# A causal convolution and a SwiGLU block in one kernel: one unit more with its convolution on ACT, DVE and POOL instead of PE, and a cast, its transposes and some copies issued sooner

## The chip, the cores and the metric

One core of a Trainium2 chip. The time is the device time of the kernel in microseconds; each changed version was run four times and the median is quoted. Ratios compare a kernel's runs with those of the kernel before in the same rounds, with a 95% interval in brackets; they are not quite the ratio of the quoted medians. A verdict of faster or slower needs 2%. The engines are named as in the profile: PE does matmuls, ACT activations, DVE and POOL elementwise work; SP issues transfers.

## The reference

A depthwise causal convolution of 7 taps (8 heads, softmax over a head's taps), then a SwiGLU block on 32768 tokens of 192 channels with 1536 hidden channels.

```python
# x: (8, 4096, 192), weight: (8, 7)
w = softmax(weight)                       # per head
out = einsum('hk,bskhg->bshg', w, windows_of_7(x))      # causal, 24 channels a head
g   = out @ w_gate                        # (32768, 192) @ (192, 1536)
y   = (silu(g) * (out @ w_val)) @ w_out   # -> (32768, 192)
```

## The kernel before

The tokens are cut into 16 units of 2048, a unit into 4 blocks of 512, a block into 12 steps of 128 hidden channels. A step is six gate/val matmuls, a SiLU on ACT, a product on DVE, and the matmuls back, which lag behind. `n` counts steps, 48 to a unit. The engines run side by side; the helper `seq` holds each of them to the order in which the program lists its instructions, step by step.

The matmuls want the convolved tokens with channels on partitions (`xc[b]`, three tiles). There are two ways to get them. Units that are not in `POOLED` have their convolution on PE (`cv` matmuls with a band matrix), and their result goes out to memory (`scr<-tm`) and back through transposing transfers. (Unit 0 has a start of its own, alike in both kernels.) Units in `POOLED` are *channel-major*:

```python
POOLED = (2, 4, 5, 6, 8, 9, 10, 12, 13, 14, 15)
...
def cast_x(u):            # POOL issues it: x to fp16 in memory, one transfer for the unit
    ... nc.gpsimd.dma_start(out=flat[...], in_=bass.AP(tensor=x_flat.tensor, ...))
def turn_x(u, i, at):     # SP issues it: the transposes that bring it in
    ... nc.sync.dma_start_transpose(out=t, in_=rows[:, at : at + P])
# a job: tap 0 and 3 on ACT, taps 1 and 2 on DVE, taps 4 to 6 and the other additions on POOL
FIRST, ON_DVE, ON_ACT, ON_POOL = 0, (1, 2), (3,), (4, 5, 6)
...
def place(u, i):          # SP issues it: the four copies that put a block's channels in place
    for dst, src in ((t1[0:Q], t0[Q:P]), (t1[Q:P], y), (t2[0:Q], y), (t2[Q:P], t0[0:Q])):
        seq(nc.sync.dma_start(out=dst, in_=src))
```

(The last lines are shortened: every slice also takes columns 0 to 511.) A unit has six jobs: a "block" job makes `pxc0` of a block, a "pair" job makes `y` for two blocks. I call the four copies a block's *slot*. Where each of these stands in the program is set by step numbers:

```python
def planned(v):
    s0 = ustep * v                        # first step of the unit, ustep = 48
    ...
    else:
        late = 12 if v == 4 else 0
        cast, jobs = s0 - 112 + late, s0 - 89
        times = range(cast + 7, cast + 27, 2)      # the eight transposes and two joins
...
# in pooled_work: a slot is placed once its jobs are done, some steps later
done = max(finished[job] for job in need)
if n < max(done + (14 if u == 2 else 18), ustep * u + NCH * i - 16):
    break
```

SP issues nearly everything that matters here from one queue: results out, transposes in, slots, `scr` writes and fetches.

## Time and profile before

| | before |
|---|---|
| median of all runs beside the change | 795.3 us (793.57 to 796.49) |
| span in the profile | 792.6 us |
| PE busy | 98% |
| one block of 512 tokens at PE's pace | 11.73 us |

The page's groups tell what one channel-major job costs. Columns: line, engine, operation, output<-inputs, shapes, count; then busy time and mean ns of one; then idle time of the engine before them.

```profile
L630 POOL TENSOR_TENSOR total<-total,piece 128x512 f32<-128x512 f32 x132 | 178.3, 1351 | 11.0
L645 POOL TENSOR_SCALAR piece<-x,both_taps 128x512 f32<-128x512 f16 x198 | 164.8, 832 | 0.0
L655 DVE SCALAR_TENSOR_TENSOR total<-x,both_taps,total 128x512 f32<-128x512 f16 x132 | 138.9, 1052 | 0.0
```

66 jobs: 3 products and 4 additions each on POOL, 2 steps on DVE. POOL carries most of it, about 8 us a job. The prediction below shows the waits and timelines.

### The profile page before, as it was taken

The numbers are of one execution on the slowest core, as the hardware profiler recorded it, in microseconds if no ns is written. First come the engines' busy times: TensorE is split into PE (matmuls) and PEld (weight loads), VectorE is DVE, ScalarE is ACT, GpSimd is POOL, SyncE is SP. The second block draws the span as 40 slices with busy tenths as digits, with TensorE's granted clock in tenths as the row PEclk, the third lists the DMA queues.
The fourth block names the chain that finished last, engine by engine and source line by source line (L and its number), as shares of the span: only waits on it lengthen the run. The fifth ranks groups of instructions, "written<-read, shape, count | busy, mean of one in ns | idle before, by whom it ended". The sixth has DMA issues, their size and how long they took to land.

```text
span 792.6 us, 27857 instructions
## 1 busy us (share of the span) xinstructions
PE 775.1 (98%) x11307; PEld 620.7 (78%) x11307; DVE 675.1 (85%) x1018; ACT 584.7 (74%) x999; POOL 551.2 (70%) x523
## 2 busy tenths in 40 slices
PE   8999999599999999999999999999999999999997
PEld 5766666477788888769889888868888888888886
DVE  6687998579999987799999997789999999997775
ACT  6666787478788876778877885687887787876664
POOL 8100797749999992069999998029999999997000
PEclk9999999889999999999999999999999999999999
DMA  9959825655352277565545219548644345221211
GB/s 135 181 121 143 159 65 108 133 126 101 75 120 79 68 109 146 117 139 99 116 96 110 65 43 181 127 112 130 117 95 107 92 92 113 69 58 45 68 55 42
DMA packets 154471, 82.38 MB, mean 104 GB/s; under 512 B 98110, under 2 KB 153798, under 8 KB 153798
## 3 DMA queue, kind: packets, MB, share of 16 engines
q1 hardware_dynamic: 136422, 64.26, 36.4%
q0 software_dynamic: 17920, 16.34, 14.1%
q8 instruction: 88, 1.44, 0.8%
q14 instruction: 41, 0.34, 0.1%
HBM read 32.68 MB, written 38.34 MB: 90 GB/s over the span
## 4 chain that ended last, share of the span: by engine, by line
PE 95%; POOL 2%; DVE 1%; DMA 1%; ACT 0%; issue 0%; SPq 0%; DVEq 0%; POOLq 0%
PE val L773 37%; PE acc L799 31%; PE gate L773 25%; POOL total L630 1%; DVE h L784 1%; PE warm L874 1%; POOL piece L645 1%; DMA pxc<-pxc 1%; PE cv L476 0%; PE turn L445 0%; PE cv L387 0%; SPq L704 0%; PE acc L820 0%; DVE total L655 0%; POOL pxc L630 0%
## 5 line engine op out<-in xcount | busy, mean ns | idle before, releaser
L782 ACT ACTIVATE sig<-gate 128x512 f16<-128x512 f32 x768 | 458.4, 597 | 189.6 <-PE gate L773 130.5
L784 DVE TENSOR_TENSOR h<-sig,val 128x512 f16<-128x512 f16 x768 | 502.6, 686 | 107.0 <-PE gate L773 65.8
L773 PEld LDWEIGHTS <-w 64*128 64x128 f16 x4608 | 354.0, 110 | 129.6 <-issue 15.5
L773 PE MATMUL gate<-pxc,w 64*128 64x512 f16 x1584 | 373.3, 377 | 9.3 <-DMA pxc<-pxc 9.2
L773 PE MATMUL val<-pxc,w 64*128 64x512 f16 x1584 | 372.4, 377 | 0.6 <-DMA pxc<-pxc 0.2
L799 PE MATMUL acc<-wo,h 64*128 64x192 f16 x6096 | 328.4, 243 | 0.5 <-issue 0.4
L799 PEld LDWEIGHTS <-h 64*128 64x128 f16 x6096 | 301.3, 94 | 28.8 <-issue 2.8
L630 POOL TENSOR_TENSOR total<-total,piece 128x512 f32<-128x512 f32 x132 | 178.3, 1351 | 11.0
L773 PE MATMUL val<-xc,w 64*128 64x512 f16 x720 | 169.6, 376 | 0.8 <-DVE h L784 0.7
L773 PE MATMUL gate<-xc,w 64*128 64x512 f16 x720 | 169.8, 376 | 0.0
L645 POOL TENSOR_SCALAR piece<-x,both_taps 128x512 f32<-128x512 f16 x198 | 164.8, 832 | 0.0
L655 DVE SCALAR_TENSOR_TENSOR total<-x,both_taps,total 128x512 f32<-128x512 f16 x132 | 138.9, 1052 | 0.0
L630 POOL TENSOR_TENSOR total<-total,part 128x512 f32<-128x512 f32 x66 | 90.7, 1375 | 66.5 <-DVE total L655 66.4
L630 POOL TENSOR_TENSOR pxc<-total,piece 128x512 f16<-128x512 f32 x44 | 58.1, 1320 | 3.7
L504 POOL COPY tm<-tm 128x1280 f16<-128x1280 f16 x4 | 5.0, 1250 | 67.2 <-DVE tm L493 67.2
L680 ACT ACTIVATE total<-x,both_taps 128x512 f32<-128x512 f16 x66 | 47.1, 714 | 0.7 <-DMA x<-xs 0.7
L680 ACT ACTIVATE part<-x,both_taps 128x512 f32<-128x512 f16 x66 | 47.1, 714 | 0.0
L858 DVE COPY o_sb<-acc 128x384 f32<-128x384 f32 x63 | 34.7, 551 | 0.0
L630 POOL TENSOR_TENSOR y<-total,piece 128x512 f16<-128x512 f32 x22 | 29.5, 1342 | 1.8
L857 ACT COPY o_sb<-acc 128x384 f32<-128x384 f32 x63 | 30.3, 480 | 0.2
L98 POOL DMA_DIRECT2D x<-in_x_dram x10 | 8.7, 884 | 24.4 <-ACT sig L782 24.4
L493 ACT CAST tm<-cv 128x480 f16<-128x480 f32 x16 | 8.2, 562 | 5.6 <-PE cv L476 5.6
(67 smaller groups left out, 85.8 us busy)
## 6 DMA issues: line engine op xcount, KB each, us to landing
out_dram<-o_sb SPq DMA_DIRECT2D x63, 384.0 KB
pxc<-pxc SPq DMA_DIRECT2D x88, 64.0 KB
pxc<-y SPq DMA_DIRECT2D x88, 64.0 KB
xs<-in_x_dram POOLq DMA_DIRECT2D x7, 768.0 KB, 7.0
x<-in_x_dram POOLq DMA_DIRECT2D x10, 480.0 KB, 10.4
scr<-tm SPq DMA_DIRECT2D x28, 130.0 KB
xs<-in_x_dram POOLq DMA_DIRECT2D x4, 774.0 KB, 8.1
x<-x SPq DMA_DIRECT2D x6, 480.0 KB
```

Source lines behind the costliest of these rows:

```text
L98: nc.gpsimd.dma_start(out=t[p0 + i0 : p0 + i1, w0 - at : w1 - at, :], in_=bass.AP(tensor=x_flat.tensor, offset=(t0 + size * w0 - pad + i0) ...
L493: eng(tm[u][:, NG * r : NG * r + NG, 2 * grp * hp : 2 * grp * hp + 2 * grp].rearrange("p g (t e) -> p g t e", t=2), banks[r][:, 0 : 2 * w] ...
L630: nc.gpsimd.tensor_tensor(job["dst"] if k == K - 1 else total, total, part, op=ALU.add)
L645: nc.gpsimd.tensor_scalar(part, shifted(k), scalar1=job["tap"][:, k : k + 1], scalar2=1.0, op0=ALU.mult, op1=ALU.mult,)
L655: nc.vector.scalar_tensor_tensor(job["total"], shifted(k), job["tap"][:, k : k + 1], job["total"], op0=ALU.mult, op1=ALU.add,)
L680: nc.scalar.activation(part, shifted(k), AF.Copy, scale=job["tap"][:, k : k + 1])
L773: nc.tensor.matmul(o, w16[m][p0 : p0 + Q, k, e::E], xc[b][k][p0 : p0 + Q, 0:TB], start=(k == 0), stop=(k == SL - 1),)
L782: silu[n] = seq(nc.scalar.activation(sg, g, AF.Silu)).ins
L784: seq(nc.vector.tensor_tensor(hj, sg, v, op=ALU.mult))
L799: nc.tensor.matmul(acc[b][bank][:, s, :], hj[p0 : p0 + Q, ts(2 * bank + s, P)], wo16[p0 : p0 + Q, j, :], start=(not second and j == 0 and ...
L857: seq(nc.scalar.copy(o_sb[:, 0:2, :], acc[b][0]))
L858: seq(nc.vector.tensor_copy(o_sb[:, 2:4, :], acc[b][1]))
```

## The change

The intent is to have less convolution on PE, the busiest engine (units 1, 3 and 8 instead of 1, 3, 7 and 11), and to bring unit 2's slots to PE in time. It does the latter by placing them sooner and by no longer holding back the cast and transposes of unit 4. All casts but unit 2's come three steps sooner (unit 4's fifteen, with the delay of twelve that goes).

```diff
-    POOLED = (2, 4, 5, 6, 8, 9, 10, 12, 13, 14, 15)
+    POOLED = (2, 4, 5, 6, 7, 9, 10, 11, 12, 13, 14, 15)
@@ planned
-            late = 12 if v == 4 else 0
-            cast, jobs = s0 - 112 + late, s0 - 89
-            times = range(cast + 7, cast + 27, 2)
+            cast, jobs = s0 - 115, s0 - 89
+            times = range(s0 - 105, s0 - 85, 2)
@@ pooled_work
-            if n < max(done + (14 if u == 2 else 18), ustep * u + NCH * i - 16):
+            if n < max(done + (12 if u == 2 else 18), ustep * u + NCH * i - 16):
```

## The prediction

> **What bounds the kernel now.** I read the page first, then the table of waits, then the timelines of PE, SP and POOL around the longest wait, and last the times of the conv matmuls. The page shows one engine full and the others not:
>
> ```profile
> PE 775.1 (98%) x11307; PEld 620.7 (78%) x11307; DVE 675.1 (85%) x1018; ACT 584.7 (74%) x999; POOL 551.2 (70%) x523
> ```
>
> In the timeline of ACT, the gate activations (L782) that open a block of 512 tokens are 11.73 us apart in almost the whole trace (from 232.89 to 244.62, for one). That is the PE's own pace; 64 blocks at it are 64 x 11.73 = 750.7 us, so only 792.6 - 750.7 = 41.9 us can be had without touching the matmuls of the FFN. Most is start and end. The rest I found by subtracting the usual step from each step: unit 2 (blocks 8 to 11) has 14 us of it, each unit with its conv on PE about 1.4, and three steps lose 0.3 to 0.9 each. The table of waits names the big one:
>
> ```profile
> PE gate L773 <- DMA pxc<-pxc: 9.2, 2, 8.7
> SPq L605 <- DMA xs<-in_x_dram: 56.2, 6, 13.5
> ```
>
> The timeline of PE shows where, and that the matmuls after it are slower (0.58 us against 0.38):
>
> ```profile
> 148.44 0.38 PE L773 MATMUL val<-pxc,w 64*128 64x512 f16 x1
> 157.49 0.58 PE L773 MATMUL gate<-pxc,w 64*128 64x512 f16 x1 [8.68 <-DMA pxc<-pxc]
> ```
>
> This is unit 2's last block. Its slot copies (L704) stand on SP's queue behind other things, as the timeline of SP shows:
>
> ```profile
> 110.09 0.58 SPq L704 DMA_DIRECT2D pxc<-pxc  x1
> 122.73 1.31 SPq L605 DMA_TRANSPOSE x<-xs  x1
> ...
> 142.99 1.27 SPq L605 DMA_TRANSPOSE x<-xs  x1
> 144.36 5.48 SPq L512 DMA_DIRECT2D scr<-tm  x8
> 149.88 5.05 SPq L520 DMA_DIRECT2D scr<-tm  x1
> 155.04 0.95 SPq L704 DMA_DIRECT2D pxc<-pxc  x1
> 156.03 1.23 SPq L704 DMA_DIRECT2D pxc<-y  x2
> 157.31 0.60 SPq L704 DMA_DIRECT2D pxc<-pxc  x1
> ```
>
> SP idles from 110.7 to 122.7, until the cast of unit 4 has landed (POOL issues it at 116.13); then it works through unit 4's transposes to 144.3, sends out unit 3's conv, is held 5.05 us in one issue that takes 0.39 to 0.45 us elsewhere, and only then reaches the slot. POOL had finished that slot's data at 134.0. The cast of unit 5 was issued at 147.88, so it was in flight during the 5.05 us.
>
> **What the Trainium skill says.** *DMA: Bandwidth & Descriptors*, "Anatomy of one DMA": "any semaphore wait happens on the issuing sequencer before dispatch", so a transfer that waits holds all behind it on its queue. The trace agrees: SP idles 12.0 us ahead of the first transpose. The same page, "Issuing engines are not separate DMA queues": transfers of all issuers share the 16 DMA engines and interleave. The 5.05 us beside a cast agree, though they do not prove it. *TensorE: Matmul & The Clock Gate*, Part 1: after an idle window of about 3.4 us the array falls to half rate, and it takes about as long to come back. The trace agrees: 0.58 to 0.63 us a matmul for some 5 us after the 8.68 us gap, and none after short gaps. *GPSIMD Engine Reference*, 3.1: a two-input operation has a floor from one read port. The trace has 1.35 us for the POOL addition against 0.83 us for its one-input product; this is why a channel-major unit costs POOL so much.
>
> **The change part by part.**
>
> 1. *One conv unit less on PE* (1, 3, 7, 11 become 1, 3, 8). It takes away 64 cv matmuls, two groups of 32 (L476), and 8 evictions. Unit 6, which holds the conv of unit 7, has blocks of 12.55 and 12.37 us instead of 11.73: 0.82 + 0.64 = 1.46 us; unit 10 has 0.78 + 0.64 = 1.42 us. Saved: **1.4 us**.
>
> 2. *One more channel-major unit.* Six jobs. DVE gains 12 x 1.05 = 12.6 us and loses 4 x 0.65; ACT gains 12 x 0.71 = 8.6 and loses 4 x 0.56. Neither bounds a block in a unit that has such jobs now (11.73 us throughout), so 0. POOL gains 6 x (2 x 1.35 + 1.38 + 1.33 + 3 x 0.83) = 47.4 us plus 0.6 for the cast, lying beside PE; but the order matters, see 4.
>
> 3. *Transposes and cast of unit 4 sooner, slots of unit 2 two steps sooner.* By the order of instructions, the cast of unit 4 now stands on POOL right after the first y (99.9 us in the trace of before) instead of after the third pxc (116.2). It can be issued at 100, land at 107 (median to landing 7.6 us, the one at 116.13 took 6.6), and SP starts unit 4's transposes 15 us earlier. From 107 I add SP's own durations in the new order (before, transposes and one slot took 122.73 to 144.3, 21.6 us): slot of block 9 issued at about 114 to 116, slot of block 10 at 128 to 130, all transposes done by 128. The conv write-out is then bound by its evictions (135), not by SP; eight issues and the ninth take 5.3 us as at other units, so slot 11 is issued at 140.5 to 143 and landed at 145, against about 147 when PE wants it. The cast of unit 5 follows job 4.0 on POOL, at about 146, after the write-out. So both waits go: block 10's steps 120 and 121 lose 1.11 + 0.44, block 11's steps 132 to 134 lose 10.24 + 0.93 + 1.06, of which the last two are the slow clock: **13.8 us**, with perhaps 1 left over. Without the earlier cast the two steps of placing alone would not do it.
>
> 4. *Casts three steps sooner.* For all later units the cast still stands on POOL after the first job of the unit before, by the order; on POOL this part moves nothing. That is the trouble: in channel-major units in a row, POOL is slower than PE. First jobs of units 12, 13, 14 start at 531.8, 581.7 and 630.7, 15 at 680.6: 49.6 us a unit against 4 x 11.73 = 46.9, so each cast comes about 2.5 us later against PE than the one before. The timelines of POOL and SP show what hangs on it:
>
> ```profile
> 589.72 0.55 POOL L590 DMA_DIRECT2D xs<-in_x_dram  x1
> 639.36 0.55 POOL L590 DMA_DIRECT2D xs<-in_x_dram  x1
> ```
>
> ```profile
> 631.87 0.59 SPq L704 DMA_DIRECT2D pxc<-pxc  x1
> 645.99 1.13 SPq L605 DMA_TRANSPOSE x<-xs  x1
> 647.22 0.52 SPq L861 DMA_DIRECT2D out_dram<-o_sb  x1
> 647.80 2.96 SPq L605 DMA_TRANSPOSE x<-xs  x2
> 650.87 0.52 SPq L704 DMA_DIRECT2D pxc<-pxc  x1
> 651.44 1.23 SPq L704 DMA_DIRECT2D pxc<-y  x2
> 652.73 0.59 SPq L704 DMA_DIRECT2D pxc<-pxc  x1
> ```
>
> SP stands from 632.5 to 645.99 for the cast of unit 15 before it can place unit 13's block 1. With 2.06 us to land (157.31 to 159.37), that slot is ready 3.1 us before PE's last use of it, and block 2's (last copy at 665.02, wanted at 669.62) 2.5 us before. One unit earlier in the run the margins are 4.2 and 3.1. Before, the longest row of channel-major units is 12 to 15. After, it is 9 to 15, and the casts of 13, 14 and 15 come third, fourth and fifth in it, where before they came first and second: margins of about 0, -2.5 and -5. PE waits about 2.5 us in unit 12 and, as PE's wait gives POOL time, 2.5 more in unit 13: **5 us added**, from 2 to 8. Gaps this short should not slow the clock. Units 4 to 7 get one cast that comes second: margin 2.5, no wait.
>
> Sum: 795.88 - 1.4 - 13.8 + 1 + 5 = 786.7; the new step losses beside casts (0.3 to 0.9 each, three before) may come or go. As either leftover may be nil, I say 785.5.
>
> **The rivals.** (a) *No drift*: SP is not held, the gain is whole, 780 to 781. For it: margins and landing vary by 1 us, and the row's first margins in units 4 and 8 (7.2 and 5.2) are better than in 12. Against: every row shows the same drift. (b) *The stall stays in unit 2*: the cast of unit 4, now at 100, falls on the slot of block 8, or SP is late again; then only part of 13.8 comes, 790 to 796. Against: slot 8 has 7 us in hand. (c) *ACT is held by POOL*: five buffers of total; in the trace of before ACT writes a buffer 14 us after POOL left it at the end of the row, against 22 at its start. Three more units take some 8, leaving 6: no wait, but if POOL slips further each wait goes straight to PE, 790 or more. (d) *DVE becomes the bound*: 85% and +10 us; blocks of 11.73 in channel-major units speak against it.
>
> **Range and chances.** The expected way has 784 to 788; (a) about one in six, (b) and (c) together about one in six. That gives 780 to 791 for eight in ten. Faster by over 2% needs 780.3 or less, that is (a) and luck with the small losses: 0.1. Slower by over 2% would need a new stall of 30 us: 0.01.
>
> **What would show it.** Right: no wait over 1 us for pxc near 135 or 148; unit 4's transposes starting near 107; conv matmuls x192; blocks of 11.73 in units 3 to 11; waits of PE for pxc of 1 to 4 us each at blocks 1 or 2 of units 12 and 13, with SP idle before the transposes of units 14 and 15. Wrong: a wait left at 148, no wait in units 12 and 13 (then the drift was overrated), or ACT idle for POOL.

## The result, and the profile after

The changed kernel takes 783.82 us (782.62 to 785.07, four runs) against 795.3; the ratio is 0.9857 (0.9831 to 0.9884). The gain of 1.4% is clear of noise. The span fell from 792.6 to 781.2 us. Line numbers after the changed place are smaller by one: L772, L781 and L783 are the old L773, L782 and L784.

The page, its first part:

```profile
PE 771.9 (99%) x11243; PEld 608.7 (78%) x11243; DVE 686.6 (88%) x1026; ACT 590.5 (76%) x1007; POOL 598.7 (77%) x565
```

The table of waits (engine and line, what it waited for; total us, times, longest):

```profile
PE val L772 <- DMA pxc<-pxc: 1.5, 4, 0.7
PE gate L772 <- DMA pxc<-pxc: 0.8, 1, 0.8
SPq L605 <- DMA xs<-in_x_dram: 118.1, 9, 19.0
```

PE's long wait is gone, and SP waits for casts twice as long as before, up to 19.0 us at once. The timeline of SP where unit 2's slots are placed:

```profile
100.52 3.35 SPq L704 DMA_DIRECT2D pxc<-pxc  x1
106.38 1.14 SPq L605 DMA_TRANSPOSE x<-xs  x1
...
127.13 0.53 SPq L704 DMA_DIRECT2D pxc<-pxc  x1
127.77 1.18 SPq L704 DMA_DIRECT2D pxc<-y  x2
128.99 0.59 SPq L704 DMA_DIRECT2D pxc<-pxc  x1
129.69 0.52 SPq L860 DMA_DIRECT2D out_dram<-o_sb  x1
134.09 5.45 SPq L512 DMA_DIRECT2D scr<-tm  x8
139.58 0.46 SPq L520 DMA_DIRECT2D scr<-tm  x1
140.14 0.62 SPq L704 DMA_DIRECT2D pxc<-pxc  x1
140.81 1.33 SPq L704 DMA_DIRECT2D pxc<-y  x2
142.19 0.60 SPq L704 DMA_DIRECT2D pxc<-pxc  x1
```

(`...` stands for lines left out.) Unit 4's transposes begin at 106.4 instead of 122.7, SP stands idle before the write-out of unit 3's convolution (130.2 to 134.1), the ninth write takes 0.46 us, and block 11's slot is out at 142.8 instead of 157.9.

The new losses stand in units 11 to 13. First two of the three late casts (units 13 and 14) on POOL's timeline, then SP's timeline, then PE's where the slot arrives:

```profile
531.13 0.55 POOL L590 DMA_DIRECT2D xs<-in_x_dram  x1
581.35 0.56 POOL L590 DMA_DIRECT2D xs<-in_x_dram  x1
```

```profile
568.47 0.59 SPq L704 DMA_DIRECT2D pxc<-pxc  x1
587.82 1.13 SPq L605 DMA_TRANSPOSE x<-xs  x1
589.06 0.53 SPq L860 DMA_DIRECT2D out_dram<-o_sb  x1
589.64 2.68 SPq L605 DMA_TRANSPOSE x<-xs  x2
592.43 1.11 SPq L704 DMA_DIRECT2D pxc<-pxc  x1
```

```profile
594.52 0.38 PE L772 MATMUL val<-pxc,w 64*128 64x512 f16 x1
595.73 0.37 PE L772 MATMUL gate<-pxc,w 64*128 64x512 f16 x1 [0.83 <-DMA pxc<-pxc]
595.91 0.37 PE L772 MATMUL val<-pxc,w 64*128 64x512 f16 x1
596.29 0.37 PE L772 MATMUL gate<-pxc,w 64*128 64x512 f16 x1
596.95 0.37 PE L772 MATMUL val<-pxc,w 64*128 64x512 f16 x1 [0.28 <-DMA pxc<-pxc]
```

SP idles 18.8 us, from 569.1 to 587.8, until the cast issued at 581.35 (unit 14's) has landed. The slot of unit 12's block 1 stands behind that. PE takes it up piece by piece; the table of waits names only part of the loss, since the weight loads that wait are put down to "issue".

To count the loss I used the starts of the 768 gate activations in the timeline of ACT: the time of each step less the usual time of the same step of a block. The losses of over 0.1 us, in us, in the profiled runs (unit 3's cv matmuls, alike in both, are left out):

| where | before | after |
|---|---|---|
| unit 2, steps 120, 121 and 132 to 134 | 13.8 | 0 |
| one unit's cv matmuls on PE (units 7 and 11 before, unit 8 after) | 1.46 + 1.42 | 1.46 |
| units 11, 12 and 13, first steps of blocks 1 and 2 | 0 | 0.45 + 3.25 + 2.07 = 5.8 |
| single steps outside unit 2, from step 48 on | 1.4 | 1.0 |

So 13.8 + 1.4 + 0.4 came back and 5.8 was lost anew, 9.8 net; the start, the end and small steps of units 0 and 2 give the rest of the 11.4 us by which the span fell. The single steps of the last row each stand 3.1 to 4.0 us behind a tap step on DVE that took 1.78 to 2.41 us, where one takes 1.05 to 1.08 on average: in the trace of before, the one at 210.4 (2.41 us) comes before the loss of 0.88 at 214.2. Other long tap steps cost nothing, and no run tests this cause.

### The profile page after: what moved, and what is told of

It reads as the page before. It is cut to its first block, busy times and chain, and to the rows that moved or that the text cites. A ratio compares the mean times of both kernels' runs of the same rounds, so it can differ in the third digit from the quotient of the medians.

```text
span 781.2 us, 27833 instructions
## 1 busy us (share of the span) xinstructions
PE 771.9 (99%) x11243; PEld 608.7 (78%) x11243; DVE 686.6 (88%) x1026; ACT 590.5 (76%) x1007; POOL 598.7 (77%) x565
## 4 chain that ended last, share of the span: by engine, by line
PE 88%; POOL 8%; issue 2%; DMA 1%; DVE 1%; ACT 0%; SPq 0%; POOLq 0%; DVEq 0%
PE val L772 35%; PE acc L798 29%; PE gate L772 22%; POOL piece L645 3%; POOL total L630 3%; POOL pxc L630 1%; DMA pxc<-pxc 1%; PE warm L873 1%; DVE h L783 0%; PE cv L476 0%; PE turn L445 0%; POOL y L630 0%; PE cv L387 0%; PE acc L819 0%; SPq L704 0%
## 5 line engine op out<-in xcount | busy, mean ns | idle before, releaser
L781 ACT ACTIVATE sig<-gate 128x512 f16<-128x512 f32 x768 | 458.6, 597 | 175.8 <-PE gate L772 115.3
L783 DVE TENSOR_TENSOR h<-sig,val 128x512 f16<-128x512 f16 x768 | 501.8, 685 | 85.3 <-PE gate L772 53.0
L772 PEld LDWEIGHTS <-w 64*128 64x128 f16 x4608 | 346.4, 110 | 130.6 <-issue 8.2
L772 PE MATMUL gate<-pxc,w 64*128 64x512 f16 x1728 | 406.1, 376 | 1.4 <-DMA pxc<-pxc 0.8
L772 PE MATMUL val<-pxc,w 64*128 64x512 f16 x1728 | 405.3, 376 | 1.8 <-DMA pxc<-pxc 1.5
L630 POOL TENSOR_TENSOR total<-total,piece 128x512 f32<-128x512 f32 x144 | 194.0, 1348 | 12.0
L645 POOL TENSOR_SCALAR piece<-x,both_taps 128x512 f32<-128x512 f16 x216 | 184.2, 853 | 0.0
L655 DVE SCALAR_TENSOR_TENSOR total<-x,both_taps,total 128x512 f32<-128x512 f16 x144 | 155.6, 1081 | 0.0
L772 PE MATMUL gate<-xc,w 64*128 64x512 f16 x576 | 135.8, 376 | 0.0
L772 PE MATMUL val<-xc,w 64*128 64x512 f16 x576 | 135.8, 376 | 0.1
L630 POOL TENSOR_TENSOR total<-total,part 128x512 f32<-128x512 f32 x72 | 97.1, 1348 | 36.6 <-DVE total L655 35.5
L630 POOL TENSOR_TENSOR pxc<-total,piece 128x512 f16<-128x512 f32 x48 | 64.8, 1351 | 4.0
```

Of the source, the lines that this page charges most:

```text
L630: nc.gpsimd.tensor_tensor(job["dst"] if k == K - 1 else total, total, part, op=ALU.add)
L645: nc.gpsimd.tensor_scalar(part, shifted(k), scalar1=job["tap"][:, k : k + 1], scalar2=1.0, op0=ALU.mult, op1=ALU.mult,)
L655: nc.vector.scalar_tensor_tensor(job["total"], shifted(k), job["tap"][:, k : k + 1], job["total"], op0=ALU.mult, op1=ALU.add,)
L772: nc.tensor.matmul(o, w16[m][p0 : p0 + Q, k, e::E], xc[b][k][p0 : p0 + Q, 0:TB], start=(k == 0), stop=(k == SL - 1),)
L781: silu[n] = seq(nc.scalar.activation(sg, g, AF.Silu)).ins
L783: seq(nc.vector.tensor_tensor(hj, sg, v, op=ALU.mult))
```

## The experiments

Eight runs in two calls; each call had its own runs of the kernel before, with medians of 794.23 and 794.52 us. All gave correct results.

**The places without the new set.** The changed kernel with one line put back:

```diff
-    POOLED = (2, 4, 5, 6, 7, 9, 10, 11, 12, 13, 14, 15)
+    POOLED = (2, 4, 5, 6, 8, 9, 10, 12, 13, 14, 15)
```

> The changed kernel with the old set of units (1, 3, 7 and 11 have their conv on PE): only the earlier cast and transposes of unit 4, the earlier slots and the casts three steps sooner remain of the change. Theory (the gain is unit 2's wait, 13.8 us; the new set saves 1.4 us and costs 5.8 us by late casts): about 781.5 us beside 795.3 of the kernel before, so 2 us or more under the changed kernel; no wait of PE for pxc over 0.3 us anywhere. Rival (the new set is where the gain comes from, the rest is worth only the wait's bare 9 us or less): 786 us or more, above the changed kernel.

Measured: 779.19 us (778.85 to 779.66), ratio 0.9808 (0.9793 to 0.9822). The table of waits has no wait of PE for pxc at all. It takes less time than the changed kernel (the intervals of the two ratios do not meet): the set, the change's headline, is what the changed kernel loses by. It is 1.2 us more than expected against its own runs of before (15.0 for 13.8); single-step losses fell too, from 1.4 to 0.5 us.

**The new set without the places.** The kernel before with the new `POOLED` alone.

> The kernel before with the new set of units only (1, 3 and 8 on PE), all else undone. Theory: unit 2 still waits some 13.8 us, one conv less saves 1.4 us, the late casts of units 13 to 15 cost some 5.8 us: about 799.7 us, slower than the kernel before by 0.5%. Rival (the set brings the gain): 790 us or less.

Measured: 799.52 us (798.35 to 800.2), ratio 1.0058 (1.0041 to 1.0076). Unit 2 loses 14.3 us, as before; units 10 to 13 lose 6.4 us at the first steps of blocks 1 and 2. Its table of waits:

```profile
PE gate L773 <- DMA pxc<-pxc: 10.0, 3, 9.3
```

```profile
SPq L605 <- DMA xs<-in_x_dram: 116.4, 9, 19.2
```

Both waits are there together, and the two halves of the change add up: 0.9808 x 1.0058 = 0.9865 against 0.9857 measured for the whole.

**Casts sooner.** The changed kernel, so that the casts stand two jobs earlier on POOL:

```diff
-            cast, jobs = s0 - 115, s0 - 89
+            cast, jobs = s0 - (127 if v >= 10 else 115), s0 - 89
```

> The changed kernel with the casts of units 10 to 15 twelve steps sooner in the program, so that each stands on POOL ahead of the last job of the unit two before instead of behind the first job of the unit before (two jobs, some 16 us earlier). Theory (SP is held by late casts, and the slots of units 11 to 13 stand behind them): SP no longer waits for these casts, the step losses at blocks 1 and 2 of units 11, 12 and 13 (5.8 us together) go, about 778 us. Rival (the losses come from POOL being late with the data itself, or from transfers that crowd each other): the losses stay or move, 782 us or more.

Measured: 778.79 us (778.16 to 778.94), ratio 0.9801 (0.9786 to 0.9815). The losses at the slots of units 11 to 13 are gone, and nothing but some 0.4 us of single steps came in their place. SP's wait for casts is less than half; it still stands 2.8 and 8.0 us for the casts of units 14 and 15, against the expectation, but at no cost to PE:

```profile
SPq L605 <- DMA xs<-in_x_dram: 47.3, 6, 14.1
```

POOL's work is the same here, and it runs later than in the changed kernel: it gives ACT the buffers of `total` back as little as 4.4 us before ACT needs them, there 11.3. Only the place of six transfers differs. Nor did the casts' own traffic crowd the slots: in the changed kernel unit 14's cast had landed (587.8) before the slot was issued (592.4). So it was the casts, and not data that POOL finished late. This version has the lowest median of all; beside the kernel before its verdict is "unclear", as 2% lies within the interval.

**Two small steps undone.** The changed kernel with `done + 14` for unit 2 and `s0 - 112` for all casts but unit 4's.

> The changed kernel with two small parts undone: the slots of unit 2 again 14 steps behind their job, and all casts but unit 4's again at 112 steps ahead. Theory (the early cast and transposes of unit 4 do the work, these two move one slot by one transpose and nothing on POOL): 783.8 us within 1.5 us, no wait of PE for pxc over 1 us before 500 us. Rival (the two steps are needed): a wait of PE of 1 us or more at block 9, 10 or 11.

Measured: 784.01 us (782.88 to 785.36), ratio 0.9869 (0.985 to 0.9887). The changed kernel's time; no loss at the slots of blocks 9 to 11. Two of the four parts that the change names are worth nothing here. The losses of units 10 to 13 remain (0.2 to 2.55 us at a step), so casts three steps sooner had not helped there either: in the order of instructions they stand behind the same POOL job with and without.

**Only unit 4.** The kernel before with one change:

```diff
-            late = 12 if v == 4 else 0
+            late = 0
```

> The kernel before with one change: the cast and transposes of unit 4 twelve steps sooner, as for any other unit. Theory (this part alone takes the wait of unit 2 away): about 15 us less than the kernel before of the same rounds, as much as the run that keeps the old set with all other parts (ratio 0.981), no wait of PE for pxc over 0.5 us. Rival (the slots also had to be placed two steps sooner): a wait of 1 us or more stays in blocks 9 to 11.

Measured: 779.25 us (778.84 to 779.75), ratio 0.9808 (0.9792 to 0.9825): the same as with all other places; the verdict is "unclear" again, for the same reason. PE has no wait for pxc.

```profile
SPq L605 <- DMA xs<-in_x_dram: 52.1, 6, 13.4
```

So the whole gain of the change, and some 4 us that it did not keep (the ratios 0.9857 and 0.9808 of 795 us), is in one constant.

**What held the ninth write.** The kernel before, with only the cast of unit 5 six steps later:

```diff
             times = range(cast + 7, cast + 27, 2)
+            if v == 5:
+                cast += 6
```

> The kernel before with the cast of unit 5 alone six steps later, so that it stands on POOL one job later and is not in flight while unit 3's conv is written out. Theory (the 5.05 us issue of the ninth write is the cast in flight): that issue takes under 1 us, the slot of block 11 is out some 4.5 us sooner, PE waits about 4 us there instead of 8.7, and the time falls by about 4.5 us against the kernel before of the same rounds. Rival (the writes fill their queue by themselves): the issue still takes about 5 us, no change of the time.

Measured: 790.09 us (788.56 to 790.92), ratio 0.9943 (0.9928 to 0.9958), 4.4 us less by the medians. The timelines of SP and PE (L775 is L773 of before):

```profile
144.00 5.37 SPq L512 DMA_DIRECT2D scr<-tm  x8
149.41 0.46 SPq L520 DMA_DIRECT2D scr<-tm  x1
149.97 0.52 SPq L704 DMA_DIRECT2D pxc<-pxc  x1
```

```profile
148.24 0.38 PE L775 MATMUL val<-pxc,w 64*128 64x512 f16 x1
151.99 0.37 PE L775 MATMUL gate<-pxc,w 64*128 64x512 f16 x1 [3.38 <-DMA pxc<-pxc]
...
153.91 0.58 PE L775 MATMUL val<-pxc,w 64*128 64x512 f16 x1
```

With no cast in flight the write takes 0.46 us instead of 5.05; that the cast held it is now shown, where the trace of before only let it be guessed. By what path it did is not. Some 4.5 of the 13.8 us in unit 2 were this collision; the rest goes with the late cast of unit 4. Other traces have such issues too, each beside a cast: a slot copy of 5.26 us at 298.6 in this run, and one of 5.55 us at 519.0 in the run with casts sooner, which cost PE nothing there. The wait of 3.38 us still slows the matmuls after it.

**Rows of 5 and 6.** The changed kernel with units 1, 3 and 9 on PE.

> The changed kernel with the third conv unit at 9 instead of 8: rows of 5 and 6 channel-major units instead of 4 and 7. Theory (each unit further in a row brings its cast 2.5 us later): no wait in unit 13; small losses (some 0.5 us) in unit 6 and in unit 12, for the third cast of a row, and some 3 us in unit 13, for the fourth cast of the row from 10; in all some 1.5 us less than the changed kernel, about 782 us. Corrected reading of the same: the fourth cast of the row from 10 is unit 15's, which holds the slots of unit 13, so the loss that stood in units 11 to 13 stands in 12 and 13. Rival (the losses belong to units 12 and 13 whatever the row): 5.8 us there as in the changed kernel, 784 us.

Measured: 782.88 us (781.73 to 784.68), ratio 0.9856 (0.9839 to 0.9874). In the trace unit 11 loses nothing at its slots and unit 13 loses 2.25 + 0.28 + 0.35 = 2.9 us: the loss stands where the fourth cast of the row from 10 holds SP; there is no fifth. (The expectation says both "no wait in unit 13" and, corrected, a loss there; the corrected reading held.) Units 6 and 12 lose 0.46 and 0.47 us, which fits the expectation in number only: they are single steps, not slots. But some 2 us of single-step losses, these included, came instead of the 1.0 of the changed kernel, and the time is the same within its spread. The place of the waits speaks for the row; the time settles nothing.

**Twelve in a row.** Only units 1 and 3 on PE, casts early enough:

```diff
-    POOLED = (2, 4, 5, 6, 7, 9, 10, 11, 12, 13, 14, 15)
+    POOLED = (2, 4, 5, 6, 7, 8, 9, 10, 11, 12, 13, 14, 15)
-            cast, jobs = s0 - 115, s0 - 89
+            cast, jobs = s0 - (139 if v >= 8 else 127 if v >= 6 else 115), s0 - 89
```

> The changed kernel with conv on PE in units 1 and 3 alone and with casts of units 6 and 7 twelve, of 8 to 15 twenty-four steps sooner: twelve channel-major units in a row without late casts. Theory (POOL needs 49.6 us a unit against PE's 46.9; ACT waits for a buffer of total once POOL is five jobs behind; with seven in a row ACT still had 4.7 us in hand): 1.4 us saved, the hand used up some two units further, then 2 to 3 us lost in each of the last three units: 783 to 786 us, PE waiting in units 13 to 15's time span with ACT idle for POOL. Rival (POOL keeps up): about 777.4 us, the best of all.

Measured: 785.63 us (785.32 to 786.16), ratio 0.989 (0.9875 to 0.9904), by the ratios some 7 us more than the version with early casts and unit 8 on PE. Its table of waits has a line that no other kernel has:

```profile
ACT total L680 <- POOL pxc L630: 15.2, 13, 2.5
```

ACT waits for POOL to give back one of five `total` buffers. While it waits, the SiLU behind it on ACT waits, and so does PE: seven times in units 11 to 14, 0.7 to 2.1 us each, sooner than the units 13 to 15 of the expectation. Over these units POOL has become the bound, although it is busy only 82% of the span.

## Why the prediction was right

The time (785.5 said, 783.82 measured) lay well within the range, and the mechanism was the one told. That the sum came so close owes something to chance: the leftover of 1 us did not come, the drift cost 0.8 us more, and 1.6 us at the start, the end and in small steps of units 0 and 2 were not in it. (Its bound for "faster", 780.3, should read 780.0, which is 0.98 x 795.88.)

- *Part 3, unit 2's wait.* Said: unit 4's transposes near 107, block 10's slot out at 128 to 130, block 11's at 140.5 to 143, wanted at 147. Measured: 106.4; 127.1 to 129.6; 140.1 to 142.8; PE came to the slot at 146.2 and did not wait. The 13.8 us all came; the 1 us that I kept as left over did not. That placing two steps sooner would not do it alone was not tested by itself, but the runs show that it is not needed (784.01 without it, 779.25 with unit 4 alone).
- *Part 1.* The trace of after has 192 cv matmuls, and one conv unit costs 1.46 us as said. It is the smallest term.
- *Part 2.* Right in the main: DVE at 88% of the span bounds no stretch. But "11.73 us throughout" was read too smoothly. The trace of before has blocks of 12.01, 12.61 and 11.98 us by the single steps that stand behind long tap steps of DVE, so this work is not quite free; they come to 1.4 us before and 1.0 after. Nor are they all "beside casts": two of the three in the trace of before have no cast in flight. The sign "blocks of 11.73 in units 3 to 11" failed for the same reason (11.91 to 12.00), for unit 7, which holds unit 8's conv (12.55 and 12.37), and for unit 11's late slot (12.18).
- *Part 4, the drift.* Said: margins of about 0, -2.5 and -5 for the casts of units 13, 14 and 15, 5 us in all, in units 12 and 13. Measured: 5.8 us; 0.45 in unit 11 already (its margin was not nil but slightly negative), 3.25 in unit 12 and 2.07 in unit 13. Two runs show the cause from both sides: it comes with the new set alone, and goes with earlier casts alone. The short gaps did not slow the clock: matmuls of 0.37 to 0.41 us right behind them.
- *The rivals.* (a) fell, as the drift was there. (b) fell: block 8's slot, beside the cast of unit 4, had its last issue stretched to 3.35 us; it was out at 103.9, and PE's first step with it began at 109.3. (c) did not bind in the changed kernel; in the version with early casts ACT's hand (the time from POOL's leaving a buffer of `total` to ACT's writing it) shrank to 4.4 us at the end of the row (about 6 said), and with twelve in a row it bound. (d) fell.

What I had not seen is what the parts mean together: by my own sum the set is worth -1.4 + 5, a loss, and I did not say that the change without its headline would be faster.

## What to carry to other kernels

A queue that issues many kinds of transfers in order is a resource of its own: a transfer that waits for something late holds everything behind it, and the fix is the place of the late producer, not a faster engine (here one constant brought 15 us). An engine that is 70% busy over the whole span can still be slower than the bound engine within a stretch; compare its time per unit with the bound's (49.6 against 46.9 us here), and multiply the difference by the length of the row before making the row longer. When a change has several parts, run each alone: here one part held the whole gain and another gave some 4 of its 15 us back.

## What the Trainium skill lacked or had wrong

- *DMA: Bandwidth & Descriptors*, "Issuing engines are not separate DMA queues", says that the sequencer's time to initiate a transfer is usually small beside the transfer. It has no number for a queue that another transfer holds up: the same 10 KB write took 5.05 us to issue beside a 774 KB cast and 0.46 us without it, and SP did nothing else meanwhile.
- *GPSIMD Engine Reference*, 3.1, gives an addition of 2048 fp32 elements (4497 ns) but none of 512: here 1.35 us on average (1.27 in most cases), and the one-input product with fp16 input took about 0.69 or 1.13 us for the same shape. In the trace of before all 63 of the long products, and 33 of the 135 short ones, overlap a tap step of DVE. Whether the read port that the page names makes the addition slower is not shown here, as the two also differ in the type of their inputs.
- *TensorE: Matmul & The Clock Gate*, Part 1, gives the idle window (about 3.4 us) but no case in which the clock falls only after PE is back at work. Here a gap of 3.38 us was enough: the granted clock was 0.50 from 152.8 us, 0.8 us after PE was back, to 159.6, with matmuls of 0.58 to 0.63 us. After the gap of 8.68 us it came back 5.4 us after PE did, later than the "about as long" of the prediction. Later than 40 us into the runs, no gate or val matmul was slow after gaps of up to 1.33 us (twelve in a row). In the trace of before the clock is 0.50 for 10.2 us (152.7 to 162.9), 0.006 of the span when halved: this fits the mean clock of 0.991 to 0.995 in the kernels with unit 2's long wait, against 0.998 to 1.0 in the others.
- No page tells how a table of waits divides a gap: for the changed kernel it gives PE 2.9 us of waits for pxc (1.5, 0.8 and 0.6) where the steps show 5.8 us lost.
